# Attention on one core: TensorE drops two of the waits in every third PV slot, and GpSimd spreads V earlier

## The chip, the cores and the metric

One core of one Trainium2 chip runs the whole kernel. The metric is the device time of one execution in microseconds (us). The kernel before takes 818.25 us (median of 4 executions, 817.39 to 819.34). The trace comes from one further execution and spans about 2 us less than the time.

## The reference

Softmax attention, 16 x 32 = 512 heads, 192 queries, 1024 keys, head width 128, all in bf16:

```python
B, H, Sq, Sk, D = 16, 32, 192, 1024, 128
scores = jnp.einsum("bhqd,bhkd->bhqk", q, k) * D ** -0.5
p = softmax(scores, axis=-1)
return jnp.einsum("bhqk,bhkd->bhqd", p, v)
```

Each K and each V is used by 192 queries only, so the kernel reads 293.6 MB and writes 25.2 MB for its work: matmuls and loads are nearly in balance.

## The kernel before

The heads are taken four at a time (a *quad*, 128 in all). Each quad has three *slots*. In a slot TensorE makes a third of the scores of one quad (`qk`) and then a third of the PV product of an earlier quad (`pv`, four slots behind). VectorE transposes K in three pieces and normalises outputs; GpSimd copies the K pieces into TensorE's layout (`order`) and V into a layout with a column of ones (`spread`); ScalarE makes the exps; the SP queue issues the loads, five buffers deep for K, Q and V.

TensorE's program is a loop, so its waits are *takes*: wait until a semaphore has a count, then take the count away. Each group begins with one to three of them:

```python
def take(s, c):
    pe.wait_ge(s, c).then_inc(s, -c)

def qk(f):
    x, b = divmod(f, 3)
    if b == 0:
        take(s_qt, 1)          # Q is transposed
    take(s_kt, 1)              # K piece is in place
    take(s_e1, 1)              # the one-bank score buffer was read by exp
    # ... 48 matmuls (b = 0, 2) or 64 (b = 1), four at a time in 32-row strips

def pv(s, part=(0, 32)):
    x, i = divmod(s, 3)
    if part[0] == 0:
        if i == 0:
            take(s_e3, 3)      # all exps of the quad
            take(s_vp, 2)      # V of the quad is spread
        if s == NF - 4:
            pe.wait_ge(s_e3, 2)
        elif s < NF - 4 or s == NF - 1:
            take(s_on, 1)      # the output bank is free
    # ... 32 matmuls
```

GpSimd and the loads:

```python
for x in range(NQ + 1):                     # GpSimd
    if x < NQ:
        for b in range(3):
            order(3 * x + b)                # waits for VectorE's transpose of piece b
    if x >= 1:
        for i in range(2):
            spread(x - 1, i)                # waits for V of quad x-1

def load_v(x, lo=0, hi=4):                  # SP queue
    if x >= NVS:
        e.wait_ge(s_pv, 3 * (x - NVS) + 2 + BLANK)
    e.dma_start(vs[:, x % NVS, lo:hi, :],
                vf[4 * x + lo:4 * x + hi].rearrange("a (m t) d -> m a (t d)", t=T)).then_inc(s_v[x % NVS], 16)
```

VectorE runs in order too: in each step it normalises one PV group (`s_on` tells TensorE) and then transposes the K piece that is needed three slots later. A late K therefore holds up the normalisations behind it.

## Time and profile before

| | before |
|---|---|
| time | 818.25 us (817.39 to 819.34) |
| TensorE, from one quad to the next (starts of the 64-matmul group, quads 8 to 124) | 6218 ns |
| of it: gap after the 64-matmul group, against the same gap elsewhere | 226 against 170 ns |
| K landing, from quad to quad (quads 12 to 126) | 6226 ns |
| loads and stores | 319.16 MB, 405 GB/s in the middle |

The last column of each row of groups tells how long an engine was idle and what ended it. These four rows are from the page of the kernel before; GpSimd (POOL) waits mostly for VectorE's transposes and just once for V:

```profile
L652 PE MATMUL f_s<-f_qt,f_kt 32*128 32x192 bf16 (+1 forms) x20528 | 422.9, 226 | 2.5 <-PEq L635 2.1
L743 DVE STREAM_TRANSPOSE f_kx<-f_kn 128x768 uint32<-128x768 uint32 (+1 forms) x384 | 334.1, 871 | 15.2 <-DMA f_kn<-in_k_dram 14.6
L607 POOL COPY f_kt<-f_kx 128x768 uint32<-128x768 uint32 (+1 forms) x384 | 301.5, 785 | 254.6 <-DVE f_kx L743 254.5
L616 POOL COPY f_vp<-f_vs 128x1024 uint32<-128x1024 uint32 x256 | 259.9, 1045 | 0.5 <-DMA f_vs<-in_v_dram 0.5
```

### The profile page before, as it was taken

The numbers are of one execution on the slowest core, as the hardware profiler recorded it, in microseconds if no ns is written. First come the engines' busy times: TensorE is split into PE (matmuls) and PEld (weight loads), VectorE is DVE, ScalarE is ACT, GpSimd is POOL, SyncE is SP. The second block draws the span as 40 slices with busy tenths as digits, with TensorE's granted clock in tenths as the row PEclk, the third lists the DMA queues.
The fourth block names the chain that finished last, engine by engine and source line by source line (L and its number), as shares of the span: only waits on it lengthen the run. The fifth ranks groups of instructions, "written<-read, shape, count | busy, mean of one in ns | idle before, by whom it ended". The sixth has DMA issues, their size and how long they took to land. (4 is left out here: it accounts for less than half of the span.)

```text
span 816.2 us, 71711 instructions
## 1 busy us (share of the span) xinstructions
PE 806.6 (99%) x32996; PEld 717.7 (88%) x32996; DVE 599.8 (73%) x1293; ACT 750.3 (92%) x772; POOL 551.0 (68%) x648
## 2 busy tenths in 40 slices
PE   8999999999999999999999999999999999999997
PEld 6888888888888888888888888888888888888886
DVE  4777777777777777777777777777777777777775
ACT  6899999999999999999999999999999999999995
POOL 5667666766766676677667667766766676676664
PEclk9999999999999999999999999999999999999999
DMA  7999999999999999999999999999999999999992
GB/s 279 399 404 405 409 404 406 408 404 406 408 403 407 408 403 409 407 403 409 406 403 409 406 404 407 405 405 392 404 401 383 397 408 403 396 409 390 393 367 70
DMA packets 138454, 319.16 MB, mean 391 GB/s; under 512 B 7216, under 2 KB 56368, under 8 KB 122160
## 3 DMA queue, kind: packets, MB, share of 16 engines
q1 hardware_dynamic: 105536, 294.22, 92.0%
q10 hardware_dynamic: 32880, 24.58, 8.9%
q14 instruction: 32, 0.26, 0.1%
q8 instruction: 6, 0.10, 0.0%
HBM read 293.60 MB, written 25.17 MB: 391 GB/s over the span
## 5 line engine op out<-in xcount | busy, mean ns | idle before, releaser
L838 ACT ACTIVATE f_pt<-f_s 128x1536 bf16<-128x1536 f32 x384 | 555.3, 1446 | 0.1
L607 POOL COPY f_kt<-f_kx 128x768 uint32<-128x768 uint32 (+1 forms) x384 | 301.5, 785 | 254.6 <-DVE f_kx L743 254.5
L679 PE MATMUL f_o<-f_vp,f_pt 128*64 128x129 bf16 x12368 | 425.7, 222 | 2.2 <-PEq L635 1.4
L652 PE MATMUL f_s<-f_qt,f_kt 32*128 32x192 bf16 (+1 forms) x20528 | 422.9, 226 | 2.5 <-PEq L635 2.1
L679 PEld LDWEIGHTS f_o<-f_vp,f_pt 128*64 128x64 bf16 x12368 | 366.1, 110 | 54.3 <-issue 29.2
L652 PEld LDWEIGHTS f_s<-f_qt,f_kt 32*128 32x128 bf16 x20528 | 348.7, 92 | 38.9 <-issue 3.3
L743 DVE STREAM_TRANSPOSE f_kx<-f_kn 128x768 uint32<-128x768 uint32 (+1 forms) x384 | 334.1, 871 | 15.2 <-DMA f_kn<-in_k_dram 14.6
L835 ACT ACTIVATE f_pt<-f_s 128x512 bf16<-128x512 f32 x384 | 229.3, 597 | 57.5 <-PE f_s L652 28.1
L616 POOL COPY f_vp<-f_vs 128x1024 uint32<-128x1024 uint32 x256 | 259.9, 1045 | 0.5 <-DMA f_vs<-in_v_dram 0.5
L764 DVE RECIPROCAL f_rinv<-f_o 128x2 f32<-128x2 f32 x381 | 64.9, 170 | 182.9 <-PE f_o L679 182.7
L768 DVE TENSOR_TENSOR f_ob<-f_o,f_rinv 128x256 bf16<-128x256 f32 x381 | 161.8, 425 | 13.3 <-DVE f_rinv L764 0.3
L752 DVE STREAM_TRANSPOSE f_qt<-f_qn 128x384 uint32<-128x384 uint32 x128 | 73.3, 573 | 0.0
L821 ACT ACTIVATE f_pt<-f_ones 128x1536 f32<-128x1536 bf16 x3 | 4.2, 1471 | 0.0
L595 POOL MEMSET f_vp<- 128x1088 uint32 (+1 forms) x3 | 3.8, 1310 | 0.0
L679 PE MATMUL f_s<-f_vp,f_pt 128*64 128x129 bf16 x96 | 3.1, 220 | 0.2 <-PEq L635 0.2
L679 PEld LDWEIGHTS f_s<-f_vp,f_pt 128*64 128x64 bf16 x96 | 2.9, 110 | 0.3 <-issue 0.3
L821 ACT ACT_TABLE_LOAD x1 | 1.3, 1283 | 1.2 <-PEq L866 1.2
L692 PE MATMUL f_o<-f_ones 128*128 128x512 bf16 x2 | 1.0, 618 | 1.1 <-POOL f_ones L592 1.1
L716 DVE MEMSET f_pt<- 128x256 uint32 x4 | 1.1, 272 | 0.9 <-PEq L866 0.9
L709 PE MATMUL f_o<-f_bad,f_ones 128*1 128x1 bf16 x1 | 0.2, 164 | 1.3 <-DVEq L810 1.3
L764 DVE RECIPROCAL f_rinv<-f_s 128x2 f32<-128x2 f32 x3 | 0.5, 171 | 1.2 <-PE f_s L679 1.2
L768 DVE TENSOR_TENSOR f_ob<-f_s,f_rinv 128x256 bf16<-128x256 f32 x3 | 1.3, 425 | 0.1
(15 smaller groups left out, 5.3 us busy)
## 6 DMA issues: line engine op xcount, KB each, us to landing
f_kn<-in_k_dram SPq DMA_DIRECT2D x127, 1024.0 KB, 18.1
f_vs<-in_v_dram SPq DMA_DIRECT2D x127, 1024.0 KB, 16.3
f_qn<-in_q_dram SPq DMA_DIRECT2D x127, 192.0 KB, 14.2
out_dram<-f_ob ACTq DMA_DIRECT2D x62, 384.0 KB, 9.5
f_vs<-in_v_dram SPq DMA_DIRECT2D x2, 512.0 KB, 6.2
f_kn<-in_k_dram SPq DMA_DIRECT2D x2, 512.0 KB, 4.4
out_dram<-f_ob SPq DMA_DIRECT2D x1, 384.0 KB, 3.0
out_dram<-f_ob SPq DMA_DIRECT2D x2, 192.0 KB, 2.2
```

The lines of the kernel that those rows point to most:

```text
L595: return gp.memset(part.bitcast(U32), 0x3F803F80)
L607: gp.tensor_copy(kt[:, x % NKT].bitcast(U32).rearrange("p U (j s u) c -> p U j s (u c)", s=2, u=2)[:, lo:hi], kx[:, x % 2].rearrange("p (U ...
L616: gp.tensor_copy(vp[:, x % NVP, 2 * T * i: 2 * T * i + 2 * T, 0:D].bitcast(U32), vs[:, x % NVS, 2 * i: 2 * i + 2, :].rearrange("p a (t d) ...
L652: ins = pe.matmul(S[:, c0: c0 + n1 - n0], kt[r, x % NKT, 2 * t + h, :, c], qt[r, x % R, h, n0:n1, c], start=w == 0 and g == 0, stop=w == 3 ...
L679: ins = pe.matmul(O[64 * z: 64 * z + 64, u, 0:129], pt[:, x % R, 2 * y + z, t * SQ + 64 * j: t * SQ + 64 * j + 64], vp[:, x % NVP, (2 * y ...
L743: dve.transpose(kx[:, x % 2].rearrange("p (U s j u) -> p s u U j", s=2, j=32, u=2)[:, :, :, lo:hi], kn[:, x % NKN].rearrange("p (s u U i) ...
L752: dve.transpose(qt[:, x % R].bitcast(U32).rearrange("p b (y j u) c -> p u y b (j c)", y=3, u=2), qn[:, x % NKN].rearrange("p (u y b i) -> ...
L764: dve.reciprocal(ri, O[:, :, 128]).then_inc(s_rc, 1)
L768: dve.tensor_tensor(ob[:, so, 6 * a + 2 * w: 6 * a + 2 * w + 2, :], O[:, :, 0:128], ri.unsqueeze(2).to_broadcast([128, 2, D]), ALU.mult,). ...
L821: return act.activation(part.bitcast(F32), ones[:, 0:1].to_broadcast([128, 2 * T * SQ // 2]), ACT_FN.Copy)
L835: act.activation(pt[:, x % R, 0, c], s1_ps[:], ACT_FN.Exp, scale=scale).then_inc(s_e1, 1)
L838: act.activation(pt[:, x % R, 1:4, c], s3_ps[f % 2][:], ACT_FN.Exp, scale=scale).then_inc(s_e3, 1)
```

## The change

The intent: exps and V need no takes of their own. The exps of a quad are done before ScalarE's exp that a later `s_e1` take waits for; and if V is spread right behind the first K piece, the take for the second K piece covers it, because GpSimd works in order.

```diff
 # GpSimd
                     if x < NQ:
-                        for b in range(3):
-                            order(3 * x + b)
+                        order(3 * x)
                     if x >= 1:
                         for i in range(2):
                             spread(x - 1, i)
+                    if x < NQ:
+                        order(3 * x + 1)
+                        order(3 * x + 2)
 # TensorE, pv
-                        if i == 0:
-                            take(s_e3, 3)
-                            take(s_vp, 2)
                         if s == NF - 4:
-                            pe.wait_ge(s_e3, 2)
+                            pe.wait_ge(s_e3, NF - 1)
                         elif s < NF - 4 or s == NF - 1:
                             take(s_on, 1)
+                        if s == NF - 3:
+                            pe.wait_ge(s_e3, NF)
+                            pe.wait_ge(s_vp, 2 * NQ)
 # ... the counts that the start gave to s_e3 and s_vp are dropped too
```

More of the change, by code (lines that the diff above doesn't have):

```diff
@@ L598, in _ @@
                 set_v(vp[:, 0, 2 * T:].rearrange("p a d -> p (a d)")).then_inc(s_blank, 1)
-                set_v(vp[:, 1].rearrange("p a d -> p (a d)")).then_inc(s_vp, 2)
+                set_v(vp[:, 1].rearrange("p a d -> p (a d)"))
                 def order(g):
@@ L824, in _ @@
                 for i in range(2):
-                    ins = blank(pt[:, 1, 2 * i: 2 * i + 2].rearrange("p a c -> p (a c)"))
-                ins.then_inc(s_e3, 3)
+                    blank(pt[:, 1, 2 * i: 2 * i + 2].rearrange("p a c -> p (a c)"))
                 for f in range(NF):
```

## The prediction

> **What bounds the kernel now.** I read the page first, then the timeline of TensorE and of the load queue, then the waits of two stretches, then the trace's own records of starts and semaphore counts.
>
> The page says TensorE 99% busy, but matmuls overlap, so I read start times instead. This is the timeline of TensorE in the middle of the run (start, length, line, operation; each row is one merged group):
>
> ```profile
> 404.02 1.10 PE L679 MATMUL f_o<-f_vp,f_pt 128*64 128x129 bf16 x32
> 405.05 1.09 PE L652 MATMUL f_s<-f_qt,f_kt 32*128 32x64 bf16 x64
> 406.16 1.10 PE L679 MATMUL f_o<-f_vp,f_pt 128*64 128x129 bf16 x32
> 407.19 1.09 PE L652 MATMUL f_s<-f_qt,f_kt 32*128 32x128 bf16 x48
> 408.21 1.10 PE L679 MATMUL f_o<-f_vp,f_pt 128*64 128x129 bf16 x32
> 409.24 1.09 PE L652 MATMUL f_s<-f_qt,f_kt 32*128 32x192 bf16 x48
> 410.26 1.10 PE L679 MATMUL f_o<-f_vp,f_pt 128*64 128x129 bf16 x32
> 411.29 1.09 PE L652 MATMUL f_s<-f_qt,f_kt 32*128 32x64 bf16 x64
> ```
>
> Groups follow each other every 1.02 to 1.03 us; only the step from an x64 group (second score piece of a quad) to the PV group after it takes longer (405.05 to 406.16, 1.11 us). That is the slot where the kernel takes three semaphores in a row (exps, V, and the output buffer). Over some 121 quads between 30 and 780 us the recorded starts give means of 1030 ns for every PV group, 1019 and 1027 ns for the two x48 groups and 1082 ns for the x64 group. The gap from the last matmul of the group to the next is 170.5 ns in the x48 group that also ends on 192 columns, and 226.6 ns (206 to 275) after the x64 group. So **the excess is 56 ns a quad**, of 6219 ns. Apart from that TensorE never stalls between 34 and 800 us.
>
> The second bound is the loads. The page's slice rows and two queue rows:
>
> ```profile
> DMA  7999999999999999999999999999999999999992
> q1 hardware_dynamic: 105536, 294.22, 92.0%
> q10 hardware_dynamic: 32880, 24.58, 8.9%
> ```
>
> The 16 engines are busy 100.9% of the span in sum. The load queue's timeline shows what that means (its rows last until the issue gets through):
>
> ```profile
> 400.35 0.82 SPq L531 DMA_DIRECT2D f_qn<-in_q_dram  x1
> 401.21 0.44 SPq L555 DMA_DIRECT2D f_vs<-in_v_dram  x1
> 401.70 5.30 SPq L546 DMA_DIRECT2D f_kn<-in_k_dram  x1
> 407.04 0.57 SPq L531 DMA_DIRECT2D f_qn<-in_q_dram  x1
> ```
>
> Each K issue takes 4 to 5 us, although the buffer it waits for had been free long before: K of quad 66 starts its issue at 395.88, and the transpose that freed its buffer ended at 390.34. V of that quad goes in 2.5 us after its buffer is free. So the queue is never short of buffers: **it is pushing against full DMA rings.** And K lands just in time. In the waits of 100 to 580 us VectorE does not wait for K at all; in those of 740 to 800 us it does:
>
> ```profile
> DVE f_kx L743 <- DMA f_kn<-in_k_dram: 2.9, 6, 0.8
> ```
>
> Landing against use, by quad: K of quad 66 lands at 413.93 and is used at 416.1 (2.2 us of slack); quad 99 0.05 us; quad 123 is waited for 0.79 us. From quad 12 (79.6) to quad 126 (789.3) K lands every 6.226 us; TensorE needs it every 6.219 us. Both run at the same pace, and neither has room.
>
> **What the Trainium skill says.** "DMA: Bandwidth & Descriptors", section "Why a DMA increments its semaphore by 16 and not by 1": up to 16 engines work on one DMA and finish independently, and only the full 16 means that all has landed. The trace agrees and shows the effect: the 16 counts of one K load are 2.1 us apart at the start (median, 20 to 100 us), 5.9 us at 250 to 400 us, 8.7 us after 600 us. The load of quad 126 has its first count at 781.4, its 13th at 782.1, its last at 789.3. A few engines, one most of all, run late, and they set when a quad may start. The same page, section "Latency and other measured facts", says that two of the engines are usually slower; the trace has no engine numbers, so it shows laggards but not which. Its section "Bandwidth" has 425 GB/s at best for large loads; here the windows give 405 GB/s over 100 to 580 us and 398 over 600 to 790.
> "Perfetto Trace Analysis", section "Tensor Engine Instruction", says that a matmul's end is an estimate: hence the starts above.
>
> **The change, part by part.**
> Removed: two of the three takes in every third PV group, 2 of 12 a quad. A take is a 51 ns record of TensorE's sequencer. In the quad shown, exps are taken at 405.717, V at 405.903, the output buffer at 406.054, and the matmul starts at 406.160: 106 ns after the last take, and a take costs some 150 to 190 ns where the sequencer has no lead. All three were satisfied before (the output semaphore at 405.804), so this is issue time, not waiting. Elsewhere even three takes cost nothing (the PV to score gap is 153 ns with two or three): the sequencer is ahead there. After the x64 group it is not.
> With one take left, the sequencer would come to it at 405.717, wait until 405.804 plus some 28 ns (as in its other slots), and the matmul could start at about 405.94, before its natural 406.078 (last start 405.908 + 170 ns). So the whole 56 ns go. Sum if TensorE alone counted: 56 ns x 126 quads = 7.1 us, to **811.1 us**.
> Moved: the V spread (two copies, 2.02 us together) goes from after the third K piece to after the first. In the timeline GpSimd would start it at about 405.5 instead of 409.64, 4.1 us earlier. V of the quad before lands 3.2 us (median; 3.1 to 5.0) after K of this one; at TensorE's present pace it is there in nearly all quads. K pieces two and three come later by up to 1 us; the second, transposed by 406.68, is copied by 408.4 and needed only at 411.29. GpSimd is 68% busy. Costs nothing while V is in time.
> Covered waits: exps and V are waited for through others that come later on the same engines; no new waits. Start and end lose a count each: nothing.
> End: the PV group at 805.02 starts 0.71 us after its natural time, with the three takes again and checks beside it. With one take, behind an output semaphore that comes at some 804.1, it would be near 804.3. **Gain at the end: about 0.7 us.** It is on the final path.
>
> **What the loads leave of it.** The last arrivals do not depend on TensorE, if the rings are full throughout. So I moved TensorE's start times forward by 56 ns a quad and asked at each quad by how much the loads hold it back. K may be late by about 0.71 us before TensorE notices: after the first transpose VectorE has 0.54 us idle before the next reciprocal, and the output take has 0.17 us of lead. V, in its new place, must land by 4.3 us after the time at which the first K piece would be transposed: 411.21 (second score piece) less 0.28 (two takes) less 2.93 (spread and copy) is 408.0, and that transpose was at 403.65. With the recorded landings, gain minus hold-up is 0.9 us at quad 24, 2.1 us at quad 64, 1.5 us at quad 96, 0.3 at quad 119 and 0.0 to 0.1 at quad 127. Of 6.7 us offered, the loads take back 6.6. With the 0.7 us of the end, **0.8 to 0.9 us remain**: 818.2 - 0.9 = 817.3, and I say 817.2 for the executions in which the loads come sooner.
>
> **Rivals.**
> A: TensorE is the only bound, all 56 ns x 126 come through, 811 us. For it: TensorE ran without a stall for 766 us, so strictly it was never held by loads; and fuller use could let the DMA engines run further ahead. Against it: K already waited for at the end, full rings, and the times before spread over 2 us (817.39 to 819.34) although TensorE's groups repeat to within a few ns: something else sets the end. Chance some 15%, with partial gains of 2 to 5 us (813 to 816) among them.
> B: the early spread makes a new wait: V late holds the second K piece on GpSimd (a strict queue), and TensorE waits for that. In my sum V is the tighter limit in a few late quads (quads 120 and 122), by 0.1 to 0.4 us. If V lags more than recorded it costs 1 to 2 us: 818 to 820. Chance 10%.
> C: the loads take it back, as above: 816.5 to 818.5. Chance 75%.
>
> **Range and chances.** C's centre is 817.3, its spread that of the times before, about 1 us either way; A's partial gains stretch the low side, B the high side. Hence 817.2, 813.8 to 818.8. Faster by 2% would be 801.9, out of reach even with all 7.1 us; slower by 2% would be 834.6, for which every quad would have to lose 130 ns. So within 2%: 0.97.
>
> **What would show it.** In the changed kernel's trace: (1) the x64 group to PV gap at 170 ns in quads that nothing holds, so a quad of about 6.163 us early on; if it stays near 226, the takes were not its cause. (2) VectorE's waits for K, 14.6 us and 12 times on the page now, many times as often, spread over the whole run and small each; GpSimd's waits for V, 0.5 us and once, likewise. If both stay rare, A holds. (3) TensorE stalls in sum of 5 to 7 us, in front of the PV group that follows the x64 group or in front of the second score group, mostly after 300 us. (4) The spread of the 16 counts no smaller, and K still landing every 6.2 us. The prediction is wrong if the late engines turn out to depend on TensorE's pace, or if the loads of the timed executions come faster than in the profiled one.

## The result, and the profile after

The changed kernel takes **817.38 us** (median of 4, 815.71 to 818.38) against 818.25 us. The ratio is 0.9987 with a 95% interval of 0.9965 to 1.0009: no difference clear of noise. (Ratios here are the mean time of one kernel's fast runs over that of the other's fast runs of the same rounds, so not quite the ratio of the medians.)

First TensorE's timeline, in the first third of the run (start, length, line, operation). Read the distance of the two x64 rows:

```profile
207.13 1.09 PE L654 MATMUL f_s<-f_qt,f_kt 32*128 32x64 bf16 x64
208.16 1.10 PE L683 MATMUL f_o<-f_vp,f_pt 128*64 128x129 bf16 x32
209.19 1.09 PE L654 MATMUL f_s<-f_qt,f_kt 32*128 32x128 bf16 x48
...
213.29 1.09 PE L654 MATMUL f_s<-f_qt,f_kt 32*128 32x64 bf16 x64
```

A quad is now 213.29 - 207.13 = 6.16 us, and the step from the x64 group to the PV group is 1.03 us, as everywhere else. So the excess is gone. But the gain did not come out at the end of the run, and the page's idle columns say where it went. These are the rows that answer to those of before:

```profile
L654 PE MATMUL f_s<-f_qt,f_kt 32*128 32x192 bf16 (+1 forms) x20528 | 423.2, 226 | 7.4 <-PEq L637 7.4
L747 DVE STREAM_TRANSPOSE f_kx<-f_kn 128x768 uint32<-128x768 uint32 (+1 forms) x384 | 334.3, 871 | 38.4 <-DMA f_kn<-in_k_dram 36.5
L616 POOL COPY f_vp<-f_vs 128x1024 uint32<-128x1024 uint32 x256 | 260.1, 1046 | 137.8 <-DMA f_vs<-in_v_dram 129.7
```

VectorE waits 36.5 us for K (14.6 before), GpSimd 129.7 us for V (0.5 before), and TensorE has new idle time in front of score groups (7.4 us; the row of before had 2.5; between 40 and 790 us it is 2.5 against none). Most waits are absorbed; the timeline around one that is not shows how a late V reaches TensorE:

```profile
618.07 2.03 POOL L616 COPY f_vp<-f_vs 128x1024 uint32<-128x1024 uint32 x2 [2.99 <-DMA f_vs<-in_v_dram]
619.71 1.10 PE L683 MATMUL f_o<-f_vp,f_pt 128*64 128x129 bf16 x32
620.04 1.44 POOL L607 COPY f_kt<-f_kx 128x768 uint32<-128x768 uint32 x2
620.64 0.98 DVE L747 STREAM_TRANSPOSE f_kx<-f_kn 128x768 uint32<-128x768 uint32 x1 [1.22 <-DMA f_kn<-in_k_dram]
621.21 1.10 PE L654 MATMUL f_s<-f_qt,f_kt 32*128 32x64 bf16 x64 [0.40 <-PEq L637]
```

GpSimd stands 2.99 us before the spread until V lands, copies V, and only from 620.04 on copies K pieces two and three, which had been transposed by 616.2 and 618.5. TensorE's PV group of 619.71 is followed by the score group for piece two at 621.21, 1.50 us later instead of 1.03. The next K, too, is 1.22 us late for VectorE. Both come from the loads.

The loads themselves are as before. From the trace's records of the 16 counts that each load adds to its semaphore:

| | K of quad 12 lands | K of quad 126 lands | per quad | first to last count, 20 to 100 us | the same, 600 to 790 us |
|---|---|---|---|---|---|
| before | 79.6 us | 789.3 us | 6.226 us | 2.2 us | 8.7 us |
| after | 80.9 us | 788.4 us | 6.206 us | 2.7 us | 8.7 us |

### The profile page after: what moved, and what is told of

Its sections match the earlier page's. It is cut to its first block, busy times and chain, and to the rows that moved or that the text cites. A ratio compares the mean times of both kernels' runs of the same rounds, so it can differ in the third digit from the quotient of the medians.

```text
span 815.0 us, 71454 instructions
## 1 busy us (share of the span) xinstructions
PE 802.2 (98%) x32996; PEld 716.0 (88%) x32996; DVE 602.0 (74%) x1293; ACT 749.9 (92%) x772; POOL 553.8 (68%) x648
## 5 line engine op out<-in xcount | busy, mean ns | idle before, releaser
L607 POOL COPY f_kt<-f_kx 128x768 uint32<-128x768 uint32 (+1 forms) x384 | 298.0, 789 | 112.6 <-DVE f_kx L747 110.3
L747 DVE STREAM_TRANSPOSE f_kx<-f_kn 128x768 uint32<-128x768 uint32 (+1 forms) x384 | 334.3, 871 | 38.4 <-DMA f_kn<-in_k_dram 36.5
L616 POOL COPY f_vp<-f_vs 128x1024 uint32<-128x1024 uint32 x256 | 260.1, 1046 | 137.8 <-DMA f_vs<-in_v_dram 129.7
```

The source lines that it names most:

```text
L607: gp.tensor_copy(kt[:, x % NKT].bitcast(U32).rearrange("p U (j s u) c -> p U j s (u c)", s=2, u=2)[:, lo:hi], kx[:, x % 2].rearrange("p (U ...
L616: gp.tensor_copy(vp[:, x % NVP, 2 * T * i: 2 * T * i + 2 * T, 0:D].bitcast(U32), vs[:, x % NVS, 2 * i: 2 * i + 2, :].rearrange("p a (t d) ...
L747: dve.transpose(kx[:, x % 2].rearrange("p (U s j u) -> p s u U j", s=2, j=32, u=2)[:, :, :, lo:hi], kn[:, x % NKN].rearrange("p (s u U i) ...
```

## The experiments

In the names, `e3` stands for the exps' semaphore `s_e3`, whose take is dropped alone, `light` for fewer bytes. The first theory, **L**: the loads set the end, at the pace of their latest DMA engines, and TensorE before the change was just as fast as they are; the 56 ns a quad are real but taken back. The rivals: **P**, TensorE alone is the bound, and the 56 ns were not what it seemed; **X**, another engine takes over; and that the early V spread costs by itself what the dropped takes win.

| run | what it is | time, us | before in the same rounds | ratio (95% interval) |
|---|---|---|---|---|
| b_light | before, a quarter of V not loaded | 819.48 | 819.53 | 1.0005 (0.9976 to 1.0033) |
| a_light | after, a quarter of V not loaded | 811.55 | 819.53 | 0.9896 (0.9874 to 0.9918) |
| e3_light | before, light V, exps' take dropped alone | 811.38 | 819.53 | 0.9906 (0.9878 to 0.9934) |
| order_only | before, GpSimd's new order alone | 819.07 | 819.53 | 0.9996 (0.9973 to 1.0018) |
| b_more | before, 1% more loads | 829.70 | 819.52 | 1.0115 (1.0095 to 1.0135) |
| e3_only | before, exps' take dropped alone | 817.90 | 819.52 | 0.9977 (0.9949 to 1.0006) |
| after_again | the changed kernel | 817.83 | 819.52 | 0.9976 (0.9953 to 0.9999) |
| e3_q15 | e3_only, each Q load cut 120 + 8 partitions | 908.86 | 819.52 | 1.1068 (1.1007 to 1.1129) |
| e3_q64 | e3_only, each Q load cut 64 + 64 partitions | 915.13 | 820.62 | one run each |

### Fewer bytes: b_light, a_light, e3_light

```diff
 # b_light on before, a_light on after: results wrong on purpose
                     if x >= NVS:
+                        hi = 3
                         e.wait_ge(s_pv, 3 * (x - NVS) + 2 + BLANK)
```

> The kernel before, with a quarter of each V load left out from quad 5 on (three of four heads, 786 KB instead of 1 MB; the result is wrong on purpose, every instruction on the five engines stays). Theory L (the loads set the end, TensorE is just as fast): TensorE's own pace of 6.219 us a quad now sets it alone, so hardly a gain: 816.3 to 817.6 us, the 56 ns after the x64 group still there, K waited for by VectorE at most in the first 35 us. Rival P (TensorE alone is the bound already): the same, 817.4 to 818.3. Rival S (loads slow TensorE itself in some hidden way): well below 815.

> The changed kernel with the same quarter of V left out. Theory L: the hidden gain comes out, 6.16 us a quad to the end, no waits for V or K after some 40 us; 809.5 to 812.5 us, the spread because the changed kernel's first quads ran up to 2.6 us later in its profile. Against b_light 5 to 7.5 us less. Rival X (the 56 ns are worth nothing because another engine, say ScalarE at 92%, takes over): within 1.5 us of b_light.

The same cut of 10% of the bytes is worth nothing to the kernel before, and it takes the changed one from 0.2% (after_again) to 1.0% below it. In the windows of a_light (TensorE, weight loads, VectorE, ScalarE, GpSimd busy; then clock, DMA share, GB/s) the loads have air, 367 and 339 GB/s instead of 405 and 398, and TensorE never rests:

```profile
100.00:580.00 480.00, 480.00 (x19957) 429.30 (x19955) 361.38 (x781) 453.23 (x468) 333.35 (x390) 1.00 1.00 367
600.00:790.00 190.00, 190.00 (x7910) 169.84 (x7904) 143.36 (x310) 179.28 (x186) 131.89 (x155) 1.00 0.92 339
```

Its quads take 6160.0 ns on average from quad 8 to 124, its 16 counts are 0.7 us apart late in the run, and no stall is left. b_light's quads take 6206.7 ns, with the excess after the x64 group still in each. The step from the x64 group to the PV group, before and after, in b_light and in a_light:

```profile
404.87 1.10 PE L653 MATMUL f_s<-f_qt,f_kt 32*128 32x64 bf16 x64
405.94 1.10 PE L680 MATMUL f_o<-f_vp,f_pt 128*64 128x129 bf16 x32
408.82 1.09 PE L655 MATMUL f_s<-f_qt,f_kt 32*128 32x64 bf16 x64
409.84 1.10 PE L684 MATMUL f_o<-f_vp,f_pt 128*64 128x129 bf16 x32
```

So the gain that the loads hid is 8 us between the medians of a_light and b_light, and 5.3 us between their profiled executions (815.3 and 810.0 us of span), whose quads differ by 47 ns x 116 = 5.4 us. The loads set the end, as theory L says, and P, X and the S of the expectation fall. That it is the *latest engines* whose pace counts is not shown by these runs. One thing did not fit: I had expected b_light at 816.3 to 817.6 us; its four executions ran 817.02, 818.06, 820.91 and 821.28. They spread by 4 us although no load was late after 40 us in its profile. So part of the spread between executions is not from the loads. The record has a candidate that no run tests: TensorE's mean granted clock was 1.000, 0.998, 0.995 and 0.995 in these four, with spans of 815.3, 816.2, 819.2 and 819.5 us, and 815.3 / 0.995 = 819.4. It would also make the 5.3 us the fairer size of the gain. In a_light the spans do not follow the clock (810.0 us at 0.999, 808.6 at 0.997).

```diff
 # e3_light: on before with the light V load
                         if i == 0:
-                            take(s_e3, 3)
                             take(s_vp, 2)
 # ... and waits at the end for the exps as in the changed kernel
```

> The kernel before with light V loads and only the take for the exps dropped; V take and GpSimd's order as before. One take of some 150 ns fewer: the last take comes at about 405.90 in the quad of the prediction, plus 106 ns, before the natural start at 406.08. Theory L: the x64 gap falls to 170 to 180 ns with one take dropped alone, and the time to 809.5 to 811 us (no lost start, since V is not asked for earlier). Rival H (each of the two takes is worth half): gap near 198, time near 813.5.

The x64 gap fell to 170 ns in every quad, and the time is that of a_light. So **one dropped take is enough**; with light loads, dropping the second and GpSimd's new order add nothing. That is what the times of the takes said: one of some 150 ns less brings the last one before the moment at which the matmul could start anyway. Rival H (half each) falls.

### The new order alone: order_only

```diff
 # on before: GpSimd's loop as in the change, all takes kept
```

> The kernel before, full loads, all takes kept, only GpSimd's order changed (V spread behind the first K piece). Theory L: end set by the loads and by TensorE's own 6.219 us: 817.5 to 819.5, GpSimd waits for V in few quads in the middle (TensorE is not ahead of the loads), in many late; x64 gap still 226. If the early spread is costly in itself (rival B of the prediction): above 820.

819.07 us, the same as before. GpSimd waits for V more often, also when TensorE is no faster than before; these are its waits for loads and VectorE's:

```profile
POOL f_vp L616 <- DMA f_vs<-in_v_dram: 26.6, 30, 1.9
DVE f_kx L745 <- DMA f_kn<-in_k_dram: 11.9, 5, 5.9
```

30 waits of at most 1.9 us, none of which stalls TensorE: the stalls between quads 8 and 124 are the old ones after the x64 group and no others. The early spread is not what takes the gain.

### More bytes: b_more

```diff
 # on before: a tile xt[128, 384], eight semaphores, and one more load a quad
+                    load_more(n)    # 16 partitions x 1536 bytes of Q, one piece on each engine
```

> The kernel before with 1% more loads: one more 24.6 KB load a quad (16 rows of 1536 bytes, one for each DMA engine, into a tile of its own that nobody reads; the result stays right). Theory L: there is no slack in the loads, so the end moves by about the time that they take at the 25 GB/s of one engine, 1536 bytes x 128 = 197 KB on each engine, 7.9 us at 25 GB/s, less whatever slack TensorE still had (1 to 2 us): 4 to 9 us slower than before. Rival P (TensorE alone is the bound): within 1 us of before.

10.2 us more between the medians, for 3.1 MB (1%). VectorE's waits for K become the rule, and TensorE stalls in front of the PV group:

```profile
DVE f_kx L756 <- DMA f_kn<-in_k_dram: 81.6, 99, 6.8
PE f_o L692 <- PEq L648: 11.5, 23, 0.9
```

So the loads had no slack even in the kernel before, in which TensorE never stalled: rival P falls a second time. I had sized it at 4 to 9 us, with the 25 GB/s of one engine (405 GB/s over 16). The packet records show why that was low: a 1536-byte packet takes 65 ns, 23.6 GB/s, and each load adds a 4-byte packet of 9 ns on each engine for the count; (65 + 9) ns x 128 = 9.5 us. The packets of the other loads took as long as before (8 KB: 315 ns against 313), so the added issue did not slow them.

### The smaller change, full loads: e3_only beside after_again

```diff
 # e3_only: on before, the edit of e3_light with full V loads
```

> The kernel before, full loads, only the exps' take dropped, GpSimd's order and the V take as before. Light loads showed that this alone closes the gap to 170 ns. Theory L: the loads set the end as in the changed kernel, 0.5 to 2 us below before, within 1.5 us of after_again; V is not waited for by GpSimd, VectorE waits for K as often as in the changed kernel (about 40 times). If the early spread costs the changed kernel something under full loads, this one is over 1.5 us faster than it.

> The changed kernel once more, to be compared with e3_only and e3_q15 on the same chip in the same rounds: 0.5 to 2 us below before.

Both are 0.2% below before (for e3_only not clear of noise), and alike: 817.90 and 817.83 us. VectorE waits for K 99 times in e3_only, not about 40 times as I had expected; the changed kernel itself has 47 such waits in its first profile and 92 in its second. They meet the same limit through different waits. In e3_only:

```profile
DVE f_kx L744 <- DMA f_kn<-in_k_dram: 65.3, 99, 4.4
PE f_o L680 <- PEq L635: 7.5, 20, 0.9
```

and in after_again:

```profile
POOL f_vp L616 <- DMA f_vs<-in_v_dram: 207.8, 124, 3.1
DVE f_kx L747 <- DMA f_kn<-in_k_dram: 60.1, 92, 5.9
PE f_s L654 <- PEq L637: 6.4, 14, 1.4
```

With V spread late (e3_only) a late K stops VectorE, that delays a normalisation, and TensorE stands before the PV group after the x64 group. With V spread early (after_again) a late V stops GpSimd, and TensorE stands before the second score group. The starts of TensorE's groups give the balance, in us between quads 8 and 124:

| | excess or stall after the x64 group | stall before the x64 group | per quad |
|---|---|---|---|
| before | 6.7, in all 116 quads | 0 | 6218.4 ns |
| after (first profile) | under 0.3 | 3.1, 8 times | 6188.9 ns |
| after_again | 1.7, 12 times | 5.3, 15 times | 6220.3 ns |
| e3_only | 8.2, 27 times | 0 | 6231.0 ns |
| a_light | 0 | 0 | 6160.0 ns |

6.7 us of small steps became 7.0 us of fewer, larger ones. (The first profile of the changed kernel had started 2.4 us later by quad 8, so it had less to give back. That was chance: about 1.5 us of it is a stretch from 26.9 to 30.3 us in which the granted clock was 0.5 and two groups took 3.53 us instead of 2.06; after_again has no such stretch and started no later than before.) And K landed on its own schedule: quad 126 at 789.3 us in before, 788.4 and 789.4 in the two of after, 790.0 in e3_only, 788.8 in order_only. The schedule is the same quad by quad: K of quads 89, 99, 109 and 119 lands 7.4 to 7.5 us after the K before it (6.2 us on average) in before, in both profiles of the changed kernel and in e3_only. The four longest stalls of TensorE in each of the three faster ones lie at quads 88, 98, 108 and 118. So the late loads came in before as well, where TensorE was slow enough not to stall. Why every tenth quad is late is not shown.

### Looking for more: e3_q15 and its control e3_q64

If the latest engine sets the pace, giving it less work should help. The Q loads are 8% of the bytes; cut in two, most of Q can be kept off the last engine.

```diff
-                e.dma_start(qn[:, x % NKN, :], ...).then_inc(s_qn[x % NKN], 16)
+                for lo, hi in ((0, 120), (120, 128)):          # e3_q64: ((0, 64), (64, 128))
+                    e.dma_start(qn[lo:hi, x % NKN, :], ...).then_inc(s_qn[x % NKN], 16)
 # ... and VectorE waits for 32 counts instead of 16
```

> e3_only with each Q load cut in two, 120 partitions and 8. By the Trainium skill (DMA: Bandwidth & Descriptors, Why a DMA increments its semaphore by 16 and not by 1) 120 partitions go on 15 engines and 8 on the first 8, so that the last engine has no Q at all, 12 KB of 156 KB a quad less. If that engine is the one that runs late, the last of the 16 counts of a K load comes 2 us or more sooner after the 13th than in e3_only (there some 7 us late in the run) and the time falls by up to 4 us, to 811 to 815 where before is at 818.3. If it is another engine, that one has as much as before or 1 KB more, and the time is the same or up to 5 us longer.

> Control for e3_q15, which was 11% slower than before instead of faster: the same two Q loads a quad and the same waits, but cut 64 and 64 partitions, so that both go on all 16 engines. If the second load a quad or its small pieces were the cost: near 909 again. If the uneven split over 15 and 8 engines was: 816 to 824, near e3_only, as b_more also had one load more a quad and lost only 10 us, all of it near the cost of its bytes.

A clear miss: 11% slower. The split over 15 and 8 engines came as expected: the loads have 55 count packets a quad instead of the 48 of e3_only (23 instead of 16 for Q, 15 + 8). The control, cut into equal halves on all 16 engines, is as slow, though in one execution of unknown state, so it is not the uneven split. It is not the count of loads either: b_more has one more load a quad too, and as many count packets as e3_q64 (64), and lost 10 us. The windows of e3_q64 show the loads at 356 GB/s while their share is as full as ever (1.04):

```profile
100.00:580.00 480.00, 424.29 (x17446) 377.03 (x17436) 314.09 (x681) 395.93 (x410) 294.38 (x341) 1.00 1.04 356
```

The packets themselves got slower: an 8 KB packet takes 364 ns on average instead of 313, a 2 KB one 101 instead of 86 (between 200 and 500 us, in the packet records of e3_q64 and of the kernel before). Longer packets alone prove little, since b_light has them too (338 and 93 ns) without a late load. Why cutting the Q load costs so much stays open, and so does which engines are late; none of these kernels beats the changed one.

## Why the prediction was right

Predicted 817.2 us (813.8 to 818.8), measured 817.38. Its steps:

- **56 ns a quad after the x64 group, from the takes' issue time, all of it won.** Shown: the gap is 170 ns in every quad of the changed kernel that nothing holds up. The reason is shown more sharply than the prediction put it, because e3_light and e3_only get it by dropping one take. Not shown is why the takes cost 207, 223, 253 and 223 ns of gap in turn in before, and 206 in nearly every quad of b_light.
- **Worth 7.1 us if TensorE alone counted.** About right: the pair with light loads shows 5.3 us between profiled executions, 8 us between medians. The excess is only 36 ns in b_light (gap 206 ns), which explains the smaller of the two; the lower clock of two b_light executions may explain the larger.
- **The loads take back 6.6 of 6.7 us.** Shown by a_light against after_again: the same program, 6160 ns a quad where the loads have room and 6220 ns where they have not; and from the other side by b_more, where 1% of bytes costs 1.2% of time.
- **V in its new place must land within 4.3 us, and is the tighter limit late in the run (rival B).** The place was right: most of TensorE's stalls are now before the second score group, and VectorE and GpSimd wait as foretold under (2). The quads were not 120 and 122 but mostly 88, 98, 108 and 118, and the 5 to 7 us of stalls of (3) came in after_again (7.0 us), not in the first profile (about 3.4 us). The size of GpSimd's waits was not foreseen (97 and 124 waits, up to 3.1 us, where the prediction spoke of small ones), but only those beyond its slack count. The cost that rival B foretold, 1 to 2 us, is not seen: e3_only, which has no early spread, ends at the same time. But with four executions each, which spread by 3.8 us (e3_only) and 2.3 us (after_again), a cost of that size can't be excluded.
- **0.7 us at the end.** Mis-sized: from the x64 group of quad 126 to the end of the span it is 19.4 us in before, 19.3 in after and 18.9 in after_again, so 0.1 to 0.4 us. The prediction blamed the three takes, but in before the take for V (804.76) came 0.02 us after GpSimd had finished spreading that V (804.74): it was a wait for the spread, and e3_only, with two takes, has the same gap of 0.88 us there. In the changed kernel that wait is gone, but TensorE stands 0.66 us (0.59 in after_again, 0.22 in before) at 800 us, in front of the last quad's first score group, until VectorE has transposed Q. VectorE's check operation before it took 0.99 and 0.92 us there, 0.54 in before; GpSimd now spreads V at that time, but that this slows it is not shown.
- **The spread of 2 us between executions as a sign of the loads.** Not a good argument: b_light, whose loads are never late after the start, spreads by 4 us. The conclusion stood on the landing times and the full rings, which held.
- **Start and end lose a count each: nothing.** Held: after_again is at quad 8 at 62.89 us, before at 63.07.

Two small readings in the prediction do not come out of the trace: the 16 counts of a K load are 5.2 us apart at 250 to 400 us, not 5.9, and V of quad 66 goes in 4.6 us after its buffer is free, not 2.5. Neither enters the sum.

The mechanism was right; that the total came within 0.2 us is luck, since the 0.7 us were too much and the whole difference is about the size of the noise: 0.9 us in the first comparison, 1.7 in the second.

## What to carry to other kernels

Before removing a small, regular bubble from a busy engine, compare its pace with the pace at which its data land, over the whole run: here both were 6.22 us a quad, so the 56 ns came back as waits elsewhere. Both kernels with a tenth of the bytes left out show what a change is worth without the loads, and 1% more bytes shows whether they have slack. And an issue cost that only shows where a queue has no lead can be gone with one instruction fewer; look at the time of each wait, not at their number.

## What the Trainium skill lacked or had wrong

- "DMA: Bandwidth & Descriptors", "Latency and other measured facts", says that two engines are usually slower, and guesses at a cause in loads issued from GpSimd; these are issued from the SP queue. It lacks that the lag can grow over a run: 2.2 us between the first and the last of a load's 16 counts at the start, 8.7 us after 600 us in the kernel before, but 0.7 us there in a_light, with a tenth fewer bytes.
- The same page, "Rules for kernel authors", says of two transfers to disjoint partition halves not to bother, since they serialize. In this stream it is worse than no use: cutting the 192 KB Q load into halves took the traffic from 404 GB/s (e3_only) to 356 and the kernel from 818 to 915 us (one execution). No run here shows the reason.
- I found no page with the cost of a wait that also takes the count away on TensorE's sequencer. In these traces two in a row are some 150 to 190 ns apart, the matmul follows 106 ns after the last where the takes hold it up (206 to 253 ns of gap), and elsewhere two or three takes leave the gap at 153 ns.
